# Two products of the second pair of f tiles moved into the first walk over D, with three f tiles of the first weights loaded at once

## The chip, the cores and the metric

One core of one Trainium2 chip. The time is device microseconds of one execution; runs are quoted by their median, and none was judged to be in a slow state (granted TensorE clock 0.999 or 1.0 in all but three runs, one each of e1, e3 and e6 below, at 0.996 to 0.997). Ratios are the mean time of one kernel's runs over the mean of the other's of the same rounds, so not quite the ratio of the medians. The span in a profile is some 1.8 us shorter than the time.

The readings come from one profiled execution of each kernel. The moment at which a load lands differs from one execution to the next, with equal loads too. The start of what is called "the train" below, which hangs on one such load, lies between 13.14 and 13.92 us in the six traces with the loads of before (mean 13.45). A difference of up to 0.8 us between two traces can therefore be chance.

## The reference

```python
# x [1, 2048, 1024], w_gate and w_up [1024, 3584], w_down [3584, 1024], all bf16
def reference(x, w_gate, w_up, w_down):
    return (gelu_tanh(x @ w_gate) * (x @ w_up)) @ w_down
```

## The kernel before

The 2048 tokens are done in two halves of 1024, each as two blocks of 512. The 3584 columns of the weights (f) are 28 tiles of 128, the 1024 of D are 8 blocks of 128. The first pair of f tiles is done by plain matmuls ("units": 64 matmuls for two f tiles, two token blocks, gate and up). Every later pair is a 2x2 block product done by Strassen's scheme in its Winograd form: 7 products of half size, M1 to M7, in place of 8. It needs sums of blocks of x ("t1" to "t4", made by VectorE with one cast on ScalarE) and of weights ("s1" to "s4", mostly by GpSimd). M1 and M2 use unsummed blocks: they are 16 bf16 matmuls on the first token block and the first f tile of the pair.

`pe`, `dve`, `act`, `sp` and `pool` fix the order of instructions on each engine. `banks` are the pieces of PSUM that TensorE writes its products to. Index `j` is 0 for gate and 1 for up. Cuts are marked with "...".

```python
FA = 2 * P                                    # two f tiles of the first weights at once
load_x0(0, sp, 0, 2); load_x0(0, act, 2, TSB) # x, D blocks 0-1, transposed on TensorE
load_w(first, 0, 0, 2, sp, 0, FA)             # gate, D blocks 0-1
load_x0(1, act)                               # x, D blocks 2-3
load_w(first, 1, 0, 2, sp, 0, FA)
load_w(first, 0, 2, 5, act, 0, FA)
load_w(first, 1, 2, 5, sp, 0, FA)
...                                           # 7 warming matmuls
load_xT(xT, 0, 0, KH, KH + 1)                 # x, D block 4, transposed by DMA, on SP
load_xT(xT, 0, 0, KH + 1, KH + 2)             # block 5
for j in range(2):
    load_w(first, j, 5, KD, act, 0, FA)       # D blocks 5-7, behind the first transpose
load_xT(xT, 0, 0, KH + 2, KD)                 # blocks 6-7
for k0, k1 in ((0, 2), (2, KH), (KH, KD)):    # x of the second 512 tokens
    load_xT(xT, 0, 1, k0, k1)
for j in range(2):
    load_w(first, j, 0, KD, sp, FA, FG)       # the other two f tiles

def first_pair_units(hT):
    held = (VB, RB)
    transpose_x0(0); ...
    part(held, 0, 0, KPQ, js=(0,))            # first 512 tokens, D blocks 0-1, gate
    transpose_x0(1)
    part(held, 0, 0, KPQ, js=(1,))
    part(held, 0, KPQ, KD)                    # the other D blocks
    t_sum("t1", 0, KH // 2); t_sum("t1", KH // 2, KH)
    for u in range(2):
        unit_out(hT, held[u], u, 0)           # gelu on ScalarE, multiply on VectorE
    held = (QB, PB)                           # fresh banks
    part(held, 1, 0, KH)                      # second 512 tokens
    t_sum("t2"); t_sum("b22"); t_sum("t3", 0, KH // 2)
    part(held, 1, KH, KD, (0,))
    unit_out(hT, held[0], 0, 1)
    t_sum("t3", KH // 2, KH)
    part(held, 1, KH, KD, (1,))
    unit_out(hT, held[1], 1, 1)
    for j in range(2):
        s_sum(0, 1, j, "s3", True, False)     # on VectorE
    for name in ("s1", "s2", "s4"):
        for j in range(2):
            s_sum(0, 1, j, name)              # on GpSimd

# pair_quads, second pair: M1, copies, M2, then M5 M5 M6 M6 M7 M7 M3 M3 M4 M4.
# t4 is made in halves: one ahead of M6's adds, one behind them.
def add_m5(dst, src):                         # VectorE; M4 needs it to be done
    dve(nc.vector.tensor_tensor(out=banks[dst][:], in0=banks[src][:],
                                in1=m5[j][:], op=ALU.add))
```

## Time and profile before

| | |
|---|---|
| time, median | 540.11 us (539.84 to 540.45, 3 runs); 539.65 with three more |
| span of the profiled execution | 538.0 us |
| TensorE busy | 532.4 us, 99% |
| second pair starts | 19.6 us |
| second pair's last product, M4, starts | 30.57 us |
| third pair starts | 32.52 us |
| each pair from the fourth on | 12.56 us (the third 10.83) |

Most of the kernel is a stream of matmuls without a gap, so anything lost or won in the first 33 us moves the end by as much. The prediction below shows the lines of this stage. GpSimd's timeline (start, length, engine, line, operation, out<-in, count, idle time before it):

```profile
18.39 4.03 POOL L385 TENSOR_TENSOR s_mem<-w_mem 128x512 fp32r<-128x512 bf16 x2 [17.08 <-DMA w_mem<-in_w_gate_dram]
22.38 3.19 POOL L385 TENSOR_TENSOR s_mem<-s_mem,w_mem 128x512 fp32r<-128x512 f32 x2
25.52 3.30 POOL L385 TENSOR_TENSOR s_mem<-w_mem,s_mem 128x512 fp32r<-128x512 bf16 x2
```

Two halves of t sums on VectorE in the same trace:

```profile
18.09 1.22 DVE L259 TENSOR_TENSOR t_mem<-xT 128x1024 fp32r<-128x1024 bf16 x1
25.06 1.59 DVE L259 TENSOR_TENSOR t_mem<-xT,t_mem 128x1024 fp32r<-128x1024 bf16 x1
```

### The profile page before, as it was taken

How to read it: one execution, taken by the hardware profiler on the slowest of the kernel's cores; microseconds unless marked ns; L12 is line 12 of the kernel's file. 1: busy time of each engine (PE TensorE's matmuls, PEld its weight loads, DVE VectorE, ACT ScalarE, POOL GpSimd, SP SyncE). 2: the span in 40 equal slices, each digit the busy share in tenths (PEclk: the TensorE clock that was granted, in tenths of full speed). 3: DMA queues.
4: the chain of work that ended last, by engine and by line, in shares of the span. 5: the costliest groups of instructions: out<-in, count | busy, mean ns of one | idle time of the engine just before them, and what ended most of it. 6: DMA issues, size and time to landing. Idle time of an engine off the chain costs nothing.

```text
span 538.0 us, 7084 instructions
## 1 busy us (share of the span) xinstructions
PE 532.4 (99%) x2352; PEld 377.9 (70%) x2388; DVE 364.2 (68%) x476; ACT 263.5 (49%) x447; POOL 244.4 (45%) x212
## 2 busy tenths in 40 slices
PE   9999999999999999999999999999999999999997
PEld 4577776666776686777776677777777766866866
DVE  1988777788775997989574334444444469969861
ACT  2555555555555329117465555555555552462280
POOL 0699877777776000000056776666777730000000
PEclk9999999999999999999999999999999999999999
DMA  9946876785815977789950405041322448677846
GB/s 205 323 128 195 207 252 185 238 262 197 291 61 200 361 239 246 237 279 308 324 171 1 156 1 158 15 142 57 100 78 80 155 133 284 220 246 252 293 141 212
DMA packets 92547, 102.70 MB, mean 191 GB/s; under 512 B 18656, under 2 KB 67424, under 8 KB 92512
## 3 DMA queue, kind: packets, MB, share of 16 engines
q1 hardware_dynamic: 69568, 80.23, 46.0%
q10 hardware_dynamic: 22944, 22.02, 13.4%
q8 instruction: 19, 0.31, 0.2%
q14 instruction: 16, 0.13, 0.1%
HBM read 85.98 MB, written 12.58 MB: 183 GB/s over the span
## 4 chain that ended last, share of the span: by engine, by line
PE 99%; issue 0%; ACT 0%; ACTq 0%
PE bank L413 63%; PE bank L703 33%; PE bank L264 3%; PE bank L202 1%; PE bank L308 0%; ACT bank L468 0%; ACT o_sb L759 0%; ACTq L468 0%
## 5 line engine op out<-in xcount | busy, mean ns | idle before, releaser
L413 PE MATMUL bank<-t_mem,s_mem 128*128 128x512 f32 x1056 | 249.6, 394 | 0.0
L413 PEld LDWEIGHTS bank<-t_mem,s_mem 128*128 128x128 f32 x1056 | 198.1, 188 | 44.1 <-DVE bank L436 0.4
L385 POOL TENSOR_TENSOR s_mem<-w_mem 128x512 fp32r<-128x512 bf16 x102 | 120.3, 1201 | 190.7 <-DVE t_mem L259 102.8
L703 PE MATMUL bank<-t_mem,s_mem 128*128 128x512 f32 (+1 forms) x548 | 127.2, 391 | 0.0
L288 DVE TENSOR_TENSOR hT<-w_mem,bank 128x512 bf16<-128x512 f32 x104 | 71.3, 687 | 79.9 <-PE bank L413 45.7
L703 PEld LDWEIGHTS bank<-t_mem,s_mem 128*128 128x128 f32 x548 | 102.4, 188 | 22.1 <-issue 0.2
L436 DVE TENSOR_TENSOR bank<-bank,m 128x512 f32<-128x512 f32 x108 | 69.9, 694 | 45.2 <-ACT m L458 43.7
L413 PE MATMUL bank<-xT,w_mem 128*128 128x512 bf16 x405 | 96.5, 380 | 1.4
L283 ACT ACTIVATE w_mem<-bank 128x512 f32<-128x512 f32 x104 | 61.8, 596 | 52.9 <-DVE bank L436 35.8
L413 PEld LDWEIGHTS <-w_mem 128*128 128x128 bf16 x432 | 40.2, 98 | 51.6 <-issue 6.8
L385 POOL TENSOR_TENSOR s_mem<-w_mem,s_mem 128x512 fp32r<-128x512 bf16 x52 | 65.8, 1285 | 0.0
L605 DVE TENSOR_TENSOR t_mem<-w_mem 128x1024 fp32r<-128x1024 bf16 x56 | 65.6, 1219 | 0.0
L385 POOL TENSOR_TENSOR s_mem<-s_mem,w_mem 128x512 fp32r<-128x512 f32 x52 | 60.9, 1192 | 0.0
L464 ACT COPY bank<-bank 128x512 f32<-128x512 f32 x54 | 30.8, 570 | 38.9 <-PE bank L413 38.9
L398 ACT CAST s_mem<-w_mem 128x512 fp32r<-128x512 bf16 x54 | 33.1, 615 | 30.6 <-PE bank L413 29.1
L675 DVE TENSOR_TENSOR s_mem<-hT 128x512 fp32r<-128x512 bf16 x52 | 34.2, 686 | 10.2 <-PE bank L703 9.4
L458 ACT COPY m<-bank 128x512 f32<-128x512 f32 x54 | 31.8, 589 | 17.5 <-PE bank L413 17.5
L703 PEld LDWEIGHTS <-hT 128*128 128x128 bf16 x224 | 21.3, 98 | 26.6 <-issue 2.1
L468 ACT COPY bank<-bank 128x512 f32<-128x512 f32 x54 | 30.7, 570 | 12.7 <-PE bank L413 12.7
L630 DVE TENSOR_TENSOR o_sb<-wd_sb,o_sb 128x512 fp32r<-128x512 bf16 x28 | 31.5, 1126 | 0.5
L768 ACT CAST o_sb<-bank 128x512 bf16<-128x512 f32 x27 | 14.8, 585 | 33.9 <-PE bank L703 33.9
L602 ACT CAST t_mem<-w_mem 128x1024 fp32r<-128x1024 bf16 x28 | 26.9, 1048 | 0.0
(45 smaller groups left out, 238.6 us busy)
## 6 DMA issues: line engine op xcount, KB each, us to landing
t_mem<-t_dram SPq DMA_DIRECT2D x56, 512.0 KB, 5.2
w_mem<-in_w_gate_dram ACTq DMA_DIRECT2D x10, 1024.0 KB, 5.5
w_mem<-in_w_up_dram ACTq DMA_DIRECT2D x10, 1024.0 KB, 5.5
wd_sb<-in_w_down_dram SPq DMA_DIRECT2D x28, 256.0 KB, 4.5
t_dram<-o_sb SPq DMA_DIRECT2D x28, 256.0 KB, 2.4
wd_sb<-in_w_down_dram SPq DMA_DIRECT2D x12, 512.0 KB, 7.7
w_mem<-in_w_down_dram SPq DMA_DIRECT2D x4, 1024.0 KB, 6.6
w_mem<-in_w_down_dram SPq DMA_DIRECT2D x8, 512.0 KB, 8.3
```

The lines of the kernel that those rows point to most:

```text
L283: act(nc.scalar.activation(out=g_sb, in_=ps[:], func=ACT.Gelu_apprx_tanh))
L288: nc.vector.tensor_tensor(out=hT[:, fc, tb * TB : (tb + 1) * TB], in0=g_sb, in1=ps[:], op=ALU.mult,)
L385: pool(nc.gpsimd.tensor_tensor(out=t, in0=in0, in1=in1, op=op))
L398: act(nc.scalar.copy(out=t, in_=a(1, 1)))
L413: nc.tensor.matmul(banks[bank][:], lhsT=lhs[:, c, :], rhs=rhs[:, c, :], start=start and c == 0, stop=c == KH - 1, skip_group_check=True,)
L436: nc.vector.tensor_tensor(out=banks[dst][:], in0=banks[src][:], in1=m5[j][:], op=ALU.add)
L458: act(nc.scalar.copy(out=m5[j][:], in_=banks[V_[j]][:]))
L464: act(nc.scalar.copy(out=banks[RB[j]][:], in_=banks[QB[j]][:]))
L605: dve(nc.vector.tensor_tensor(out=t, in0=in0, in1=in1, op=ALU.subtract))
L630: dve(nc.vector.tensor_tensor(out=t, in0=in0, in1=in1, op=ALU.subtract))
L675: dve(nc.vector.tensor_tensor(out=t, in0=in0, in1=in1, op=op))
L703: nc.tensor.matmul(banks[bank][:, c0:c1], lhsT=lhs(i, u), rhs=rhs(i)[:, c0:c1], start=start and i == 0, stop=stop and i == NS - 1, skip_gr ...
```

## The change

Its intent: while the first blocks of x arrive, each landed block should feed more matmuls. M1 and M2 of the second pair use the same x blocks as the units of the first 512 tokens, so they are done in the same walk over D. For this the third f tile has to come with the first two. The fourth comes with them for D blocks 5 to 7, and late for the others.

```diff
-    FA = 2 * P
+    FA = 3 * P
+    KA = 5
...
-        load_w(first, j, 5, KD, act, 0, FA)
+        load_w(first, j, KA, KD, act)                # all four f tiles, D blocks 5-7
...
-        load_w(first, j, 0, KD, sp, FA, FG)
+        load_w(first, j, 0, KA, sp, FA, FG)          # fourth f tile, D blocks 0-4
...                                                   # copies of x's transposes all on VectorE
-        held = (VB, RB)
+        held = (PB, RB)
+        def m12(j, k0, k1):                          # M1 into QB, M2 into VB
+            for kd in range(k0, k1):
+                pe(nc.tensor.matmul(banks[(QB, VB)[kd // KH][j]][:], ...))
...
-        part(held, 0, 0, KPQ, js=(1,))
-        part(held, 0, KPQ, KD)
...                                                   # M1 of D blocks 0-1
+        for j in range(2):
+            part(held, 0, KPQ, KH, js=(j,))
+            m12(j, KPQ, KH)
+            act(nc.scalar.copy(out=banks[VB[j]][:], in_=banks[QB[j]][:]))
+        for kd in range(KH, KD - 2):
+            part(held, 0, kd, kd + 1)
+            for j in range(2):
+                m12(j, kd, kd + 1)
...
         for u in range(2):
             unit_out(hT, held[u], u, 0)
-        held = (QB, PB)
-        part(held, 1, 0, KH)
+        for j in range(2):
+            m12(j, KD - 2, KD)
+        unit_out(hT, VB, 2, 0)                       # the multiply of M2, now ahead of t2
+        for j in range(2):
+            part(held, 1, 0, KH, js=(j,))            # the same banks again
         t_sum("t2")
...                                                   # pair_quads: M1 and M2 left out for this pair
```

More of the change, by code (lines that the diff above doesn't have):

```diff
@@ L303, in transpose_x0 @@
             parts = [(0, 0, 2), (0, 2, 4), (1, 0, 4)]
-        for n, (kd, ts0, ts1) in enumerate(parts):
-            tp = banks[(PB + QB)[(2 * q + n) % 4]][:].bitcast(BF16)
+        else:
+            parts.reverse()
+        for bank, (kd, ts0, ts1) in zip((PB[1], RB[1], QB[1])[q:], parts):
+            tp = banks[bank][:].bitcast(BF16)
             for ts in range(ts0, ts1):
@@ L314, in transpose_x0 @@
             cols = slice(ts0 * P, ts1 * P)
-            if q == 0 or n == 0:
-                dve(nc.vector.tensor_copy(out=xT[0][:, kd, cols], in_=tp[:, cols]))
-            else:
-                act(nc.scalar.copy(out=xT[0][:, kd, cols], in_=tp[:, cols]))
+            dve(nc.vector.tensor_copy(out=xT[0][:, kd, cols], in_=tp[:, cols]))
     def part(held, tb, k0, k1, us=(0, 1), js=(0, 1)):
@@ L326, in first_pair_units @@
     def first_pair_units(hT):
-        held = (VB, RB)
+        held = (PB, RB)
+        def m12(j, k0, k1):
+            for kd in range(k0, k1):
+                pe(
+                    nc.tensor.matmul(
+                        banks[(QB, VB)[kd // KH][j]][:],
+                        lhsT=block((0, "p", 1), j, 0, kd // KH)[:, kd % KH, :],
+                        rhs=xT[0][:, kd, :],
+                        start=kd == 0,
+                        stop=kd in (KH - 1, KD - 1),
+                        skip_group_check=True,
+                    )
+                )
         transpose_x0(0)
-        warm(RB[1], TB // 2)
+        warm(PB[0], TB // 2)
         part(held, 0, 0, KPQ, js=(0,))
+        m12(0, 0, KPQ)
         transpose_x0(1)
-        part(held, 0, 0, KPQ, js=(1,))
-        part(held, 0, KPQ, KD)
+        for u in range(2):
+            part(held, 0, 0, KPQ, (u,), (1,))
+        m12(1, 0, KPQ)
+        for j in range(2):
[7 more added lines that the diff above has]
+        for j in range(2):
+            part(held, 0, KD - 2, KD, js=(j,))
         t_sum("t1", 0, KH // 2)
@@ L338, in first_pair_units @@
             unit_out(hT, held[u], u, 0)
-        held = (QB, PB)
-        part(held, 1, 0, KH)
+        for j in range(2):
+            m12(j, KD - 2, KD)
+        unit_out(hT, VB, 2, 0)
+        for j in range(2):
+            part(held, 1, 0, KH, js=(j,))
         t_sum("t2")
@@ L464, in do_m6 @@
             act(nc.scalar.copy(out=banks[RB[j]][:], in_=banks[QB[j]][:]))
-        for j in range(2):
-            mm(P_[j], j, block(key, j, 0, 0), b11, True)
-            act(nc.scalar.copy(out=banks[QB[j]][:], in_=banks[P_[j]][:]))
         behind = len(pending) > 0
         eager = not behind and "m2" in then
+        if not eager:
+            for j in range(2):
+                mm(P_[j], j, block(key, j, 0, 0), b11, True)
+                act(nc.scalar.copy(out=banks[QB[j]][:], in_=banks[P_[j]][:]))
         if behind:
@@ L482, in pair_quads @@
         elif eager:
-            m2()
             done("m2")
```

## The prediction

> **What bounds the kernel now.** I read the page first (busy time and groups), then the chain of work at the start, then the table of stretches, then the timelines of VectorE and of the weight loads in the first 33 us, the only stage that the change touches.
>
> ```profile
> PE 532.4 (99%) x2352; PEld 377.9 (70%) x2388; DVE 364.2 (68%) x476; ACT 263.5 (49%) x447; POOL 244.4 (45%) x212
> ...
> L413 PE MATMUL bank<-t_mem,s_mem 128*128 128x512 f32 x1056 | 249.6, 394 | 0.0
> ```
>
> TensorE is busy 99% of 538.0 us, so time goes down only if matmuls are removed or a wait of TensorE is. In the raw trace a bf16 matmul of 512 columns starts every 216 ns (the 38 below: 8.36 us / 38 = 0.220, one record missing), and an f32 one every 227 ns. Once the pairs run behind each other, one takes 12.56 us, every time: 40 x 0.2267 + 16 x 0.2159 = 12.52. Nothing is to be had there.
>
> ```profile
> 6.55 4.43 PE bank L264 x20
> 10.98 0.02 issue
> 11.00 0.38 PE bank L264
> 11.38 0.05 issue
> 11.43 8.36 PE bank L264 x38
> ```
>
> In this chain of the start TensorE hardly waits either. Start to start, the matmul at 7.35 is 0.11 us late (weights landed 7.31), the one at 11.00 is 0.19 us late (the transpose of x for D blocks 6 and 7 landed 10.96). So the start waits 0.3 us in all, though it lives from hand to mouth: each load lands within half a microsecond of its use.
>
> ```profile
> 2.00:6.00 4.00, 4.00 (x20) 1.87 (x19) 0.96 (x3) 0.24 (x1) 0.00 (x0) 1.00 1.01 272
> 6.00:11.00 5.00, 4.98 (x29) 2.26 (x28) 0.42 (x1) 1.63 (x2) 0.00 (x0) 1.00 1.28 245
> 11.00:16.00 5.00, 4.94 (x23) 2.28 (x24) 3.68 (x5) 1.43 (x3) 0.00 (x0) 1.00 0.91 201
> 16.00:20.00 4.00, 4.00 (x20) 1.83 (x19) 4.00 (x4) 2.82 (x6) 1.61 (x1) 1.00 1.14 322
> 20.00:26.00 6.00, 5.95 (x28) 3.86 (x27) 6.00 (x6) 4.16 (x8) 6.00 (x5) 1.00 1.09 359
> ```
>
> The table of stretches (columns: length, then busy PE, PEld, DVE, ACT, POOL, clock, DMA share, GB/s) shows two other limits: the DMA engines are full from 2 to 11 us (share over 1), and VectorE is busy all of 16 to 26 us.
>
> ```profile
> 13.54 1.23 DVE L259 TENSOR_TENSOR t_mem<-xT,xT 128x1024 fp32r<-128x1024 bf16 x1 [0.19 <-DMA xT<-in_x_dram]
> ...
> 27.57 0.70 DVE L436 TENSOR_TENSOR bank<-bank,m 128x512 f32<-128x512 f32 x1 [0.22 <-ACT bank L464]
> 28.18 1.73 DVE L259 TENSOR_TENSOR t_mem<-xT,t_mem 128x1024 fp32r<-128x1024 bf16 x1
> 29.83 1.28 DVE L436 TENSOR_TENSOR bank<-bank,m 128x512 f32<-128x512 f32 x2
> ```
>
> ```profile
> 26.67 0.76 PEld L413 LDWEIGHTS bank<-t_mem,s_mem 128*128 128x128 f32 x4 [0.17 <-ACT bank L464]
> 27.59 2.59 PEld L413 LDWEIGHTS bank<-t_mem,s_mem 128*128 128x128 f32 x12 [0.15 <-ACT bank L464]
> 30.57 1.69 PEld L413 LDWEIGHTS bank<-t_mem,s_mem 128*128 128x128 f32 x8 [0.40 <-DVE bank L436]
> ```
>
> This is what I rest on. VectorE starts the second half of the sum t1 at 13.54, when x of the second 512 tokens has landed (13.42), and then works without a pause, but for 0.22 us, to the add that ends at 30.52. M4 of the second pair starts at 30.57, on that add. The two waits for ACT before are about 0.13 us each beyond the usual pace, the one for VectorE 0.36 us.
>
> **What the Trainium skill says.** "TensorE: Matmul & The Clock Gate", Back-to-back issue gap, gives N/2.4 + 2.5 ns, 216 ns for 512 columns; the trace has 216. "DMA: Bandwidth & Descriptors", Issuing engines are not separate DMA queues, says that DMAs from SP and ACT share the same 16 engines and interleave; the trace agrees, the total staying at 272 and 245 GB/s while both queues move data. The same page, Latency and other measured facts, gives 261 GB/s for a DMA transpose that cannot concatenate; in the trace they reach about 290 at best. "SBUF — State Buffer", Who interferes with whom, says that a VectorE instruction with two SBUF inputs contends with a GpSimd one that reads SBUF; the halves of t sums take 1.23 us before GpSimd starts (18.39) and 1.58 to 1.73 beside it.
>
> **The change, part by part.**
> (1) *Arithmetic.* M1 and M2 of the second pair are 16 matmuls, moved ahead, not removed. The order of instructions of both programs shows the same number of rows on TensorE. Work saved: none. The 32 matmuls of the first 512 tokens become 48 done in one walk over D, so each landed block of x feeds 6 matmuls in place of 4.
> (2) *Weights.* The first loads carry 3 f tiles in place of 2, and blocks 5 to 7 of D all 4. Extra before the transposes of the second 512 tokens: 2 x 65.5 KB (blocks 0, 1), 2 x 98.3 KB (2 to 4), 2 x 196.6 KB (5 to 7) = 721 KB. The late loads shrink by the same. At 322 to 359 GB/s, which plain weight loads reach in the last two stretches, that is 2.0 to 2.2 us of full DMA time.
> (3) *Does TensorE starve?* Needs after the change: first matmul 4.85 as before; blocks 2, 3 at 4.85 + 0.21 (cold) + 12 x 0.216 + 0.45 (transposes) = 8.1; block 4 at 10.7; block 5 at 12.0, its up weights 12.4; block 6 at 13.3. Arrivals, each moved by the extra bytes that I count in front of it: gate weights 2 to 4 at 7.3 + 0.8 = 8.1; up weights 5 to 7 at 10.1 + 2.0 = 12.1; x blocks 6, 7 at 10.96 + 1.9 = 12.9. So the need moves out about as far as the supply: no large wait, with 0.3 to 0.4 us to spare, and the old 0.3 us gone. That alone would save up to 0.3 us.
> (4) *VectorE.* The x of the second half comes behind all of it. On SP's own queue 229 KB are added ahead of it (0.7 us at 330 GB/s), on both 721 KB (2.2 us). I take 1.5 us: t1's second half starts at 15.0, not 13.54. VectorE's sequence from there to the add that M4 waits for has the same instructions (one multiply has moved forward, which changes no sum): 30.52 - 13.54 - 0.22 = 16.76 us of work. 15.0 + 16.8 = 31.8. The t4 half would end after GpSimd's burst and can win back up to 0.5 us: 31.3 to 31.8, against 30.52. TensorE arrives there at about 30.0, and waits. Cost: 0.8 to 1.3 us, which covers the early savings rather than adding to them.
> (5) *Banks.* The second 512 tokens now write the same banks (0, 1, 6, 7) as the first; before they had fresh ones. Four matmuls of M2 (0.86 us) and 8 more lie between, and gelu and multiply take 0.60 and 0.68 us each. The multiplies stand behind t1's second half: 15.0 + 1.23 + 2 x 0.65 = 17.5; bank 1 is needed at about 17.6. That holds narrowly.
> (6) *GpSimd.* It waits for the fourth tile, which lands about when it did (18.3, 20.0): later in the queue, but 164 KB in place of 524. No change. ACT swaps two bank copies for two others and loses one copy of x. No change.
> Sum: -0.3 at the start, which the later wait absorbs, and about +1.0 from VectorE: 540.1 + 1.0 = 541.1 if all of this holds.
>
> **The rivals.** *A, the plain gain:* the extra bytes hide, x of the second half lands as before, and the 0.3 us at the start and part of the 0.36 us before M4 vanish: 539.5. For it: the late weights get smaller, so GpSimd may start sooner and be out of VectorE's way; between 11 and 16 us DMA is not full (0.91). Against: it is full until 11. *B, TensorE starves:* the ACT queue, which gets 490 KB of the extra, falls behind, and the up weights of blocks 5 to 7 or the gate weights of 2 to 4 come 0.5 us or more after 12.4 and 8.1: 541 to 541.5, visible as a wait between 8 and 13.5 us. For it: 0.3 us to spare is less than my error. *C, mine:* VectorE's train starts late and M4, perhaps M3 too, waits. *D, C and the banks:* the full 2.2 us of delay, and the multiplies hold bank 1 too: 542.
>
> **Range and chances.** A at 0.3, B at 0.2, C at 0.4 (541.1), D at 0.1. Weighed: 0.3 x 539.5 + 0.2 x 541.2 + 0.4 x 541.1 + 0.1 x 542 = 540.7, and I round up to 540.8, as C is what I can show. None moves the time by 1%, and 2% is 10.8 us, the time of 48 matmuls, which are neither added nor removed. Runs of before spread by 0.6 us. Predicted 540.8, range 539.4 to 542.1; faster by over 2% 0.01, within 0.98, slower 0.01.
>
> **What would show it.** Right: the same count of matmuls; x of the second half landing 1 to 2 us later; t1's second half starting near 15.0; the add before M4 of the second pair ending past 31.2 with TensorE waiting over 1 us on it or on the adds before M3; pairs of 12.56 us from then on. Wrong: M4 of that pair starting before 30.5 (A), or a wait of over 0.5 us between 8 and 13.5 us (B). If any pair after the second runs at another pace, I have misread the whole.

## The result, and the profile after

The changed kernel takes 542.71 us (542.42 to 544.09, 6 runs), the kernel before 539.65 us (539.11 to 540.45, 6 runs): ratio 1.006, 95% interval 1.0046 to 1.0074. That is about 3 us slower, 0.6%. It lies within 2%, as I said, but outside my range, which ended at 542.1.

The profiled execution was the slowest of the six (544.09 us). Its span is 4.3 us longer than that of before. 3.4 us of it are there when the third pair starts; 0.8 us more are one late load near 493 us that the other traces do not show. The pairs from the fourth on again take 12.56 us each.

The stretches (columns as in the prediction: length, busy PE, PEld, DVE, ACT, POOL, clock, DMA share, GB/s):

```profile
6.00:11.00 5.00, 5.00 (x29) 2.50 (x28) 0.76 (x2) 1.01 (x2) 0.00 (x0) 1.00 1.22 242
11.00:16.00 5.00, 5.00 (x24) 2.15 (x23) 1.18 (x1) 1.65 (x3) 0.00 (x0) 1.00 1.08 215
26.00:33.00 7.00, 5.51 (x22) 3.83 (x23) 7.00 (x7) 1.66 (x3) 6.01 (x4) 1.00 0.32 116
```

TensorE does not starve up to 16 us. DMA is now full to 16 us (share 1.08, where it was 0.91), and in that stretch VectorE works 1.18 us in place of 3.68. From 26 to 33 us VectorE is busy all the time while TensorE is idle for 1.5 us of 7.

VectorE's timeline (L260 is the line of the t sums, L259 before; L465 the adds, L436 before):

```profile
16.31 1.22 DVE L260 TENSOR_TENSOR t_mem<-xT,xT 128x1024 fp32r<-128x1024 bf16 x1 [0.26 <-DMA xT<-in_x_dram]
17.45 1.88 DVE L289 TENSOR_TENSOR hT<-w_mem,bank 128x512 bf16<-128x512 f32 x3
19.24 2.28 DVE L260 TENSOR_TENSOR t_mem<-xT,t_mem 128x2048 fp32r<-128x2048 bf16 x1
21.45 2.18 DVE L260 TENSOR_TENSOR t_mem<-xT 128x1024 fp32r<-128x1024 bf16 x1
...
28.80 2.19 DVE L260 TENSOR_TENSOR t_mem<-xT,t_mem 128x1024 fp32r<-128x1024 bf16 x1
30.91 1.28 DVE L465 TENSOR_TENSOR bank<-bank,m 128x512 f32<-128x512 f32 x2
32.11 1.21 DVE L260 TENSOR_TENSOR t_mem<-xT,t_mem 128x1024 fp32r<-128x1024 bf16 x1
33.24 1.28 DVE L465 TENSOR_TENSOR bank<-bank,m 128x512 f32<-128x512 f32 x2
```

I call "the train" what VectorE does from the start of t1's second half to the end of the first add of the last row above, which frees the bank that M4 writes. Before it ran from 13.54 to 30.52 us, 16.98 us long. Now it runs from 16.31 to 33.93, 17.62 us, with no pause in it. The start moved by 2.77 us and the length by 0.64: together the 3.41 us by which the third pair starts later (35.93 against 32.52). Two halves of sums that took 1.22 and 1.59 us take 2.18 and 2.19 (the first half of t3, the first of t4). A third, t4's second half, took 1.73 and takes 1.21; the 0.64 us is what is left of all these and of shorter pauses.

The weight loads on TensorE show its waits in the second pair:

```profile
24.70 0.76 PEld L442 LDWEIGHTS bank<-t_mem,s_mem 128*128 128x128 f32 x4 [0.30 <-POOL s_mem L414]
26.80 0.76 PEld L442 LDWEIGHTS bank<-t_mem,s_mem 128*128 128x128 f32 x4 [1.33 <-POOL s_mem L414]
28.37 1.69 PEld L442 LDWEIGHTS bank<-t_mem,s_mem 128*128 128x128 f32 x8 [0.81 <-POOL s_mem L414]
...
33.98 1.69 PEld L442 LDWEIGHTS bank<-t_mem,s_mem 128*128 128x128 f32 x8 [0.58 <-DVE bank L465]
```

M4 starts at 33.98, on VectorE's add, as before. But TensorE also waits three times for GpSimd's sums (L414, L385 before), which it did not do before. GpSimd's timeline:

```profile
19.36 5.29 POOL L414 TENSOR_TENSOR s_mem<-w_mem 128x512 fp32r<-128x512 bf16 x2 [18.06 <-DMA w_mem<-in_w_gate_dram]
24.61 3.71 POOL L414 TENSOR_TENSOR s_mem<-s_mem,w_mem 128x512 fp32r<-128x512 f32 x2
28.29 3.73 POOL L414 TENSOR_TENSOR s_mem<-w_mem,s_mem 128x512 fp32r<-128x512 bf16 x2
```

The six sums start 1.0 us later, and take 12.7 us in place of 10.4. The first of the six alone, and the second:

```profile
19.36 3.18 POOL L414 TENSOR_TENSOR s_mem<-w_mem 128x512 fp32r<-128x512 bf16 x1 [18.06 <-DMA w_mem<-in_w_gate_dram]
22.50 2.15 POOL L414 TENSOR_TENSOR s_mem<-w_mem 128x512 fp32r<-128x512 bf16 x1
```

Read beside VectorE's lines, the two engines take turns. t2 ends at 21.53; GpSimd's first sum, begun before, ends 1.02 us after that, at 22.55; the first half of t3, begun at 21.45, ends 1.08 us after that, at 23.63; GpSimd's second sum ends 1.02 us after that, at 24.65. It goes on so to the end of GpSimd's work at 32.01: six turns of GpSimd of 1.01 to 1.03 us and five of VectorE's sums (three of 1.08, two of 0.55 us) add up to the whole 10.49 us. VectorE's multiplies and adds, which read one operand from PSUM, take no turn: 0.67 to 0.69 us beside GpSimd and 0.68 alone.

So the trace leaves several candidates: the late x (L), the order and the banks (O), the port to SBUF at which VectorE and GpSimd take these turns (P), and GpSimd's sums being late for TensorE (G).

### The profile page after: what moved, and what is told of

Same layout as the page of the kernel before. It is cut to its first block, busy times and chain, and to the rows that moved or that the text cites.

```text
span 542.3 us, 7127 instructions
## 1 busy us (share of the span) xinstructions
PE 536.4 (99%) x2388; PEld 377.9 (70%) x2388; DVE 365.0 (67%) x477; ACT 262.8 (48%) x446; POOL 246.5 (45%) x212
## 4 chain that ended last, share of the span: by engine, by line
PE 95%; DVE 2%; DMA 1%; issue 1%; ACT 0%; DVEq 0%
PE bank L442 61%; PE bank L732 31%; PE bank L265 1%; DMA t_mem<-t_dram 1%; DVE t_mem L260 1%; PE bank L333 1%; PE bank L203 1%; DVE hT L289 0%; DVE s_mem L412 0%; DVE bank L465 0%; PE bank L311 0%; ACT o_sb L788 0%; DVEq L289 0%; DVEq L260 0%
## 5 line engine op out<-in xcount | busy, mean ns | idle before, releaser
L414 POOL TENSOR_TENSOR s_mem<-w_mem 128x512 fp32r<-128x512 bf16 x102 | 121.6, 1213 | 192.1 <-DVE t_mem L260 103.0
L465 DVE TENSOR_TENSOR bank<-bank,m 128x512 f32<-128x512 f32 x108 | 69.8, 694 | 44.9 <-ACT m L487 43.7
L442 PE MATMUL bank<-xT,w_mem 128*128 128x512 bf16 x416 | 94.3, 380 | 0.0
L442 PEld LDWEIGHTS <-w_mem 128*128 128x128 bf16 x416 | 38.6, 98 | 49.7 <-issue 6.8
L414 POOL TENSOR_TENSOR s_mem<-w_mem,s_mem 128x512 fp32r<-128x512 bf16 x52 | 66.3, 1301 | 0.0
L414 POOL TENSOR_TENSOR s_mem<-s_mem,w_mem 128x512 fp32r<-128x512 f32 x52 | 61.2, 1198 | 0.0
L493 ACT COPY bank<-bank 128x512 f32<-128x512 f32 x54 | 30.8, 570 | 40.7 <-PE bank L442 40.7
L500 ACT COPY bank<-bank 128x512 f32<-128x512 f32 x52 | 29.6, 570 | 11.7 <-PE bank L442 11.7
```

Of the source, the lines that this page charges most:

```text
L414: pool(nc.gpsimd.tensor_tensor(out=t, in0=in0, in1=in1, op=op))
L442: nc.tensor.matmul(banks[bank][:], lhsT=lhs[:, c, :], rhs=rhs[:, c, :], start=start and c == 0, stop=c == KH - 1, skip_group_check=True,)
L493: act(nc.scalar.copy(out=banks[RB[j]][:], in_=banks[QB[j]][:]))
```

## The experiments

All times of one batch stand beside the kernel before on the same chip. Fourteen kernels ran. "Train" is read from each trace as above. Six runs compute a wrong result on purpose, marked in the table; the other eight are correct.

| run | early bytes added | train starts | train length | third pair starts | time, us | ratio (95% interval) |
|---|---|---|---|---|---|---|
| before | 0 | 13.54 | 16.98 | 32.52 | 539.65 | |
| changed | 721 KB | 16.31 | 17.62 | 35.93 | 542.71 | 1.0060 (1.0046 to 1.0074) |
| e1_loads_only | 721 KB | 15.69 | 17.03 | 34.72 | 542.33 | 1.0049 (1.0024 to 1.0074) |
| d_half_dose | 393 KB | 14.66 | 17.02 | 33.68 | 541.07 | 1.0028 (1.0013 to 1.0043) |
| e2_order_only (wrong) | 0 | 13.47 | 19.28 | 34.76 | 542.31 | 1.0039 (1.0023 to 1.0055) |
| p_before (wrong) | 0 | 13.21 | 16.98 | 32.47 | 539.58 | 0.9997 (0.9980 to 1.0014) |
| p_after (wrong) | 721 KB | 16.37 | 14.39 | 33.09 | 540.15 | 1.0011 (0.9996 to 1.0025) |
| p_order (wrong) | 0 | 13.43 | 16.95 | 32.70 | 539.21 | 0.9994 (0.9979 to 1.0009) |
| q_after (wrong) | 721 KB | 16.20 | 17.62 | 35.82 | 543.57 | 1.0070 (1.0055 to 1.0085) |
| q_order (wrong) | 0 | 13.14 | 19.29 | 34.43 | 542.30 | 1.0049 (1.0032 to 1.0066) |
| e3_weights_first | 721 KB | 15.45 | 17.62 | 35.08 | 542.88 | 1.0062 (1.0032 to 1.0092) |
| e4_mult_late | 721 KB | 15.56 | 17.29 | 34.85 | 542.61 | 1.0051 (1.0034 to 1.0068) |
| e5_fourth_late | 524 KB | 14.78 | 17.60 | 34.39 | 541.69 | 1.0039 (1.0022 to 1.0056) |
| e6_fourth_ahead | 1049 KB | 18.75 | 16.17 | 36.95 | 543.75 | 1.0077 (1.0062 to 1.0092) |
| b3_weights_first | 0 | 14.26 | 17.02 | 33.28 | 540.12 | 1.0010 (0.9995 to 1.0025) |
| b4_mult_late | 0 | 13.92 | 16.96 | 32.88 | 539.65 | 1.0001 (0.9986 to 1.0016) |

### The loads alone

```diff
 # kernel before
-    FA = 2 * P
+    FA = 3 * P
+    KA = 5
-        load_w(first, j, 5, KD, act, 0, FA)
+        load_w(first, j, KA, KD, act)
-        load_w(first, j, 0, KD, sp, FA, FG)
+        load_w(first, j, 0, KA, sp, FA, FG)
```

> The order of the kernel before with the loads of the changed one. If the larger early loads are the cause (theory L: x of the second 512 tokens lands late, VectorE's train starts late, M4 of the second pair waits), nearly the whole loss is here: 542 to 543 us, t1's second half starting near 16. If the order of the matmuls and the re-used banks are the cause (theory O): 539.5 to 540.

Measured: 542.33 us. The third pair starts 2.20 us later. The train starts 2.15 us later (15.69), and its length is the old one (17.03). That the length is the same is the sum of changes that cancel: t3's first half is stretched here too, while the pause of 0.22 us is gone and t4's second half is short (1.21 us).

```profile
20.23 2.18 DVE L260 TENSOR_TENSOR t_mem<-xT 128x1024 fp32r<-128x1024 bf16 x1
28.18 1.60 DVE L260 TENSOR_TENSOR t_mem<-xT,t_mem 128x1024 fp32r<-128x1024 bf16 x1
```

TensorE had even waited 1.9 us for x of D block 5, which landed at 12.32, and that wait cost nothing on top: the train had not reached M4 by then. L holds for the loads, with GpSimd's sums in place.

### Half of the extra bytes

```diff
 # kernel before
-        load_w(first, j, 5, KD, act, 0, FA)
+        load_w(first, j, 5, KD, act)
-        load_w(first, j, 0, KD, sp, FA, FG)
+        load_w(first, j, 0, 5, sp, FA, FG)
```

> The kernel before with all four f tiles of blocks 5 to 7 loaded early: 393 KB more ahead of x of the second 512 tokens, against 721 in the run with all loads of the change. If bytes set the landing: t1's second half at 14.6 to 15.0 (13.5 before, 15.7 with all), and 540.7 to 541.3. If bytes are not it, but the slow service of ACT's large packets beside transposes: as late as with all, 15.5, as the large packets on ACT are all here, and 542.

Measured: 541.07 us, the train starting at 14.66. In the order of before, three doses (0, 393, 721 KB) give starts at 13.54, 14.66 and 15.69, lengths of 16.98, 17.02 and 17.03, and third pairs at 32.52, 33.68 and 34.72. In these traces each microsecond of delay of x delays the third pair by about one. The bytes on both queues count in full: 393 KB / 1.12 us = 351 GB/s, 721 KB / 2.15 us = 335 GB/s, the rate of plain weight loads in the table of stretches (322 to 359). From the means of all traces with these loads, the delay of 721 KB is 16.03 - 13.45 = 2.6 us (280 GB/s), so the rate is known only roughly. The large packets on ACT are all in this dose, and about half the bytes gave about half the delay, so they need no explanation of their own.

### The order alone

```diff
 # changed kernel; the loads of before, and
-    lhsT=block((0, "p", 1), j, 0, kd // KH)[:, kd % KH, :],
+    lhsT=block((0, "p", 0), j, 0, kd // KH)[:, kd % KH, :],
```

> The order of the changed kernel with the loads of before; M1 and M2 of the second pair take the weights of another f tile that is there early, so the result is wrong on purpose. Theory L: 539.2 to 540.0, t1's second half near 13.5. Theory O: 542 or more.

Measured: 542.31 us, against L. x landed as before and the train starts at 13.47, but it is 19.28 us long. VectorE's timeline:

```profile
15.12 1.91 DVE L288 TENSOR_TENSOR hT<-w_mem,bank 128x512 bf16<-128x512 f32 x3 [0.43 <-PE bank L264]
16.95 2.29 DVE L259 TENSOR_TENSOR t_mem<-xT,t_mem 128x2048 fp32r<-128x2048 bf16 x1
19.15 2.18 DVE L259 TENSOR_TENSOR t_mem<-xT 128x1024 fp32r<-128x1024 bf16 x1
21.74 0.69 DVE L288 TENSOR_TENSOR hT<-w_mem,bank 128x512 bf16<-128x512 f32 x1 [0.41 <-ACT w_mem L283]
22.34 2.19 DVE L259 TENSOR_TENSOR t_mem<-xT 128x1024 fp32r<-128x1024 bf16 x1
```

The multiplies of the first 512 tokens stand ahead of t2, and with 12 more matmuls ahead of them on TensorE they wait for it (0.43 us). A third multiply has joined them. So t2 starts at 16.95, not 15.88. GpSimd starts its sums at 17.89 here. Before, the first half of t3 began at 18.09, ahead of GpSimd, and took 1.22 us. Here it begins at 19.15, behind GpSimd's start, and takes 2.18. By the start of the third pair the order costs 2.2 us by itself, and the loads 2.2 us by themselves; together 3.4 us, not 4.4. The two costs overlap: the stretch of t3's first half is in both runs and counts once, and a late x hides the wait for TensorE (in the changed kernel the multiplies wait for nothing).

With x late, what the order adds is one item. Between e1 (17.03 us) and the changed kernel (17.62) every entry of the train agrees to 0.05 us but two: the multiply of M2, 0.6 us, stands ahead of t2 and no longer between s3 and t4's first half, and that half takes 2.19 us, not 1.60. Where the multiply stood it ran in a turn of GpSimd's and cost nothing; ahead of t2, where GpSimd has not begun, it costs its own length.

That VectorE's sums are longer because GpSimd is in the way was so far read off one trace's times. The next runs test it.

### GpSimd's six sums taken away

```diff
+    for name in ("s1", "s2", "s4"):
+        for j in range(2):
+            pool(nc.gpsimd.memset(s_fixed(j, name).bitcast(F32), 0.01))   # at the start
...
-                s_sum(0, 1, j, name)
+                ssum[(0, 1, j, name)] = s_fixed(j, name).rearrange("p (a b) -> p a b", b=P)
```

The tiles that M5, M6 and M3 of the second pair read are constants set in the first microseconds, so GpSimd does nothing from then until the third pair's sums, and the result is wrong. This was done to the kernel before, the changed one, and the one with the order alone.

> The kernel before, with GpSimd's six sums for the second pair (s1, s2, s4) taken away: those tiles are set to a constant at the start, so the result is wrong on purpose. Theory P: from 18 to 32 us VectorE's train of sums is stretched by GpSimd, which holds up each VectorE instruction with two SBUF inputs, and that stretched train sets M4 of the second pair. Then the train here ends 1.5 to 2.5 us sooner, and the time falls only by the 0.36 us that M4 waits: 539.0 to 540.0. Theory L (the landing of x alone matters): the same as before.

> The changed kernel with the same six sums taken away (wrong on purpose). Theory P: t1's second half still starts near 16, but the train then takes about 14 us in place of 17.6, M4 starts at 30 to 31, and the time is 539.5 to 540.5, nearly all of the loss gone. Theory L: at most 0.7 us of the loss goes, 542 or more.

> The run with the changed order and the loads of before, with the same six sums taken away (wrong on purpose). Theory P: the order alone costs 2.2 us because the multiplications of the first 512 tokens wait for TensorE, push t2 and t3 into GpSimd's sums and so stretch the train; without those sums 539.0 to 540.0. If the order costs in another way (banks, TensorE's own order): still 541.5 or more.

Measured: 539.58, 540.15 and 539.21 us. The changed kernel loses 0.11% in place of 0.60%, and the order alone 0 in place of 0.39%. VectorE's timeline in p_after:

```profile
21.51 1.22 DVE L260 TENSOR_TENSOR t_mem<-xT 128x1024 fp32r<-128x1024 bf16 x1
...
26.30 1.22 DVE L260 TENSOR_TENSOR t_mem<-xT,t_mem 128x1024 fp32r<-128x1024 bf16 x1
...
30.07 1.29 DVE L475 TENSOR_TENSOR bank<-bank,m 128x512 f32<-128x512 f32 x2
```

x is as late as ever (the train starts at 16.37), but the train is 14.39 us long, not 17.62, because the sums take 1.22 us again. In p_before the train should have ended at least 1.5 us sooner, and it ended only 0.3 us sooner (30.19), all of it from an earlier start. Pauses filled its length: VectorE waits 1.06 us for TensorE and 1.47 us for ScalarE, which are then the slower ones. So in the kernel before GpSimd's sums had already used up VectorE's slack, and any delay of the train showed.

These runs took away two things at once: GpSimd's use of the port, and TensorE's waits for its sums. They also give VectorE some 3 us of slack, in which a late start or another wait can hide; so they show that the loss needs GpSimd's sums, and not that the sums are all of it. No run has the late x in the old order without the sums.

### The port kept busy, the waits taken away

```diff
 # p_after, p_order
+                idle_sum(j, name)     # the same six sums on GpSimd, into tiles nobody reads
                 ssum[(0, 1, j, name)] = s_fixed(j, name).rearrange(...)
```

> The changed kernel with GpSimd doing the same six sums at the same time, but into tiles that nobody reads; TensorE reads constants set at the start, as in the runs without the sums (wrong on purpose). So the shared port is as busy as ever, and no wait of TensorE for GpSimd is left. Theory P (the port stretches VectorE's train, and the train sets M4): train 17 to 17.6 us, 542.2 to 543. Theory G (TensorE's waits for GpSimd's late sums set the time): as without the sums, 540.2.

> The same for the changed order with the loads of before (wrong on purpose). Theory P: train 18.5 to 19.3 us, 541.3 to 542.5. Theory G: 539.2.

Measured: 543.57 and 542.30 us, the full loss again. In q_after:

```profile
28.69 2.19 DVE L260 TENSOR_TENSOR t_mem<-xT,t_mem 128x1024 fp32r<-128x1024 bf16 x1
31.60 1.69 PEld L470 LDWEIGHTS bank<-t_mem,s_mem 128*128 128x128 f32 x8 [1.96 <-issue]
33.87 1.69 PEld L470 LDWEIGHTS bank<-t_mem,s_mem 128*128 128x128 f32 x8 [0.58 <-DVE bank L493]
```

TensorE no longer waits for GpSimd at all, and reaches M3 sooner, to wait there 1.9 us in q_after (the view names no releaser; M3 starts 0.12 us after an add on VectorE ends, as in the changed kernel and in e2). The trains have the old lengths to 0.01 us (17.62 and 19.29). G is refuted. P is shown: GpSimd's work beside VectorE's sums, and not the arrival of what it makes, is what the loss needs. The constants that TensorE reads are the same as in the p runs, so they are not what took the loss away there. That it is GpSimd's reading of SBUF that collides, and not its writing, no run separates.

### Attempts to shorten the train or to speed up the loads

```diff
 # e3: changed kernel; b3: the same in the kernel before
+    for j in range(2):
+        load_w(first, j, KA, KD, sp)
     load_xT(xT, 0, 0, KH, KH + 1)
...
-        load_w(first, j, KA, KD, act)
```

> The changed kernel with the weights of blocks 5 to 7 issued from SP ahead of the transposes of x, not from ACT beside them. If the part of the delay that I did not foresee (2.8 us measured against 2.2 us of bytes) comes from transposes and weights being served side by side (theory M), x of the second half lands 1 to 2 us sooner and the time is 540.5 to 541.7. If bytes alone count: 542.5 or more, as the bytes ahead of that x are the same.

> The kernel before with the weights of blocks 5 to 7 issued from SP ahead of the transposes. x of blocks 6 and 7 lands 0.3 to 1 us sooner, as it did in the changed kernel, x of the second half at most 0.5 us sooner: 539.2 to 539.8, the 0.19 us wait for x gone if block 4 does not come late (after 9.1).

Measured: 542.88 us in the changed kernel. x of D blocks 6 and 7 came 1.3 us sooner (12.12), but x of the second half only 0.85 us sooner than in the profile of the changed kernel and 0.2 us sooner than in e1, whose loads are those of the changed kernel. The larger of the two is about what traces with equal loads differ by, and the time did not improve. So the gain of 1 to 2 us from no longer serving transposes and weights side by side did not show. In the kernel before the same move gave 540.12 us, no gain, with x of the second half 0.7 us later (14.14), where I had expected it at most 0.5 us sooner.

```diff
 # e4: changed kernel; b4: the same in the kernel before
-        unit_out(hT, VB, 2, 0)
+        g_m2 = gelu(banks[VB[0]])
+        late.append(lambda: mult(hT, g_m2, banks[VB[1]], 2, 0))   # run behind M7's adds
```

> The changed kernel with the multiplication of the second pair's M2 output moved from ahead of t2 to behind the adds of M7, out of VectorE's train. If the train sets the start of M4 (theory L): about 0.6 us faster, 542.1. If the sums on GpSimd set it (theory G), or the banks: no change, 542.7.

> The kernel before with the multiplication of the second pair's M2 output moved out of VectorE's train, behind the adds of M7. If the count of VectorE instructions in the train sets M4: its 0.36 us of waiting goes and the time is 539.2. If the port shared with GpSimd sets it: the multiplication, which reads PSUM, is no port work, the wait stays within 0.2 us, and the time is as before.

Measured: 542.61 and 539.65 us. Taking a multiply of 0.68 us out shortens the train by 0.33 us in the changed kernel and by 0.02 us in the one before. In the changed kernel 0.2 us of it became a wait, because t2's x had not landed. In the kernel before, t4's first half began 0.6 us sooner, counted from the start of the train, and met more of GpSimd's sum: 2.19 us in place of 1.59. The multiply reads one operand from PSUM and had run beside GpSimd at no cost. The time moves less than a run's noise; it is the trace that decides. I had expected 0.6 us from it in the changed kernel.

```diff
 # e5: changed kernel, the fourth f tile late for all D blocks
-    KA = 5
+    KA = KD
-        load_w(first, j, KA, KD, act)
+        load_w(first, j, 5, KD, act, 0, FA)
 # e6: changed kernel, the late weights ahead of x of the second 512 tokens
-    for k0, k1 in ((0, 2), (2, KH), (KH, KD)):
-        load_xT(xT, 0, 1, k0, k1)
     for j in range(2):
         load_w(first, j, 0, KA, sp, FA, FG)
+    for k0, k1 in ((0, 2), (2, KH), (KH, KD)):
+        load_xT(xT, 0, 1, k0, k1)
```

> The changed kernel with the fourth f tile late for all blocks of D: 197 KB fewer ahead of x of the second 512 tokens, the same bytes more behind it. Theory L (landing of x): t1's second half 0.5 to 0.7 us sooner, near 15.5, and the time 542.0. Theory P (landing and shared port together): GpSimd's sums also start later, near 20, which takes back part: 542 to 543.

> The changed kernel with the late weights (the fourth f tile) loaded ahead of x of the second 512 tokens. Theory L: that x lands about 1 us later still, 543.5 to 544. Theory P: GpSimd starts some 3 us sooner, so more of its sums are done before the train meets them: 542 to 543, no worse than the changed kernel.

Measured: e5 takes 541.69 us. 197 KB fewer ahead of x, and the train starts at 14.78, as long as before the edit (17.60). GpSimd did not start later (18.49, where I had expected 20), so what I expected to be taken back was not. e6 takes 543.75 us, as L said and against what I wrote for P. GpSimd starts at 15.48 and the train is shorter (16.17), but it starts at 18.75. Also, TensorE waits 2.6 us at 18.7 us for the multiply that frees bank 1. So an earlier start of GpSimd does not pay for a later x.

No version beat the kernel before beyond the noise. The changed kernel's best variant (e5) still loses 0.4%.

## Why the prediction was wrong

By its own steps:

- **What bounds the kernel**, and that the only stage to look at is the first 33 us: right. The pairs from the fourth on kept 12.56 us. One reading was too general: not every load landed within half a microsecond of its use (x of D block 4 landed at 8.06 and was used about 9.1). It did no harm. The bound inside that stage was named as well: VectorE's train from the landing of x to M4. Every run shows M4 starting within 0.1 us of the end of the train, except the three without GpSimd's sums, in which TensorE is the slower one.
- **(1) and (3), matmuls and starving**: right that TensorE does not starve. In the profile after, TensorE up to 16 us waits once, 0.15 us, for x of D block 5 (landed 12.74). The up weights of blocks 5 to 7 landed at 12.66, where I had 12.1, and x of blocks 6 and 7 at 13.38, not 12.9. They were in time because TensorE itself was late: four of its first matmuls started 427 ns apart, where before only one did, which is 0.6 us. A wait of this size (1.9 us in e1) did not reach M4 in any case. Rival B is out.
- **(4), the delay of x, failed in size.** I had 0.7 us from the bytes on SP's own queue and 2.2 us from the bytes on both, and took 1.5 in between. Measured: 2.77 us in the profiled execution, 2.15 in e1 with the same loads, 2.6 in the mean of the five traces with them. The two-queue figure was the right term. The page that I quoted says that the queues share the 16 engines, and I had seen the engines full up to 11 us, so nothing spoke for the middle. d_half_dose shows that the ACT queue's bytes count in full.
- **(4), the length of the train, failed outright.** I took 16.76 us of work as a constant ("one multiply has moved forward, which changes no sum") and let up to 0.5 us of it be won back. It was 17.62. The 0.5 us was won (t4's second half, 1.21 in place of 1.73 us), but t3's first half lost 0.96 us and t4's first half 0.60. The durations in it depend on whether GpSimd is at the port at that moment, which I had quoted from the SBUF page myself without using it. x came 2.8 us later and GpSimd began only 1.0 us later, which put the first half of t3 behind GpSimd's start (e1 has this too). And the moved multiply did change a sum: t4's first half now waits out the turn of GpSimd in which the multiply used to run. The order alone costs 2.2 us (e2). Without GpSimd's sums that cost is not there (p_order: 0), with them it is all back (q_order). Not all of it is longer sums: e2's trace also has two waits of VectorE, 0.43 us for TensorE and 0.41 for ScalarE, which the slack of p_order can hide.
- The end of the train was therefore 33.93 and not 31.3 to 31.8. Of the 2.1 to 2.6 us missing, 1.3 are the start (16.31 against 15.0) and 0.8 to 1.4 the length (17.62 against 16.76, or 16.3 with the win-back).
- **(5), banks**: held, as I had it, narrowly; only in e6, with x later still, did bank 1 make TensorE wait.
- **(6), GpSimd, "no change"**: wrong. It started 1.0 us later and its six sums took 12.7 us in place of 10.4, for the same reason seen from the other side.
- **Rivals**: C was the right mechanism as far as the late train goes, at a size beyond D's; the sums stretched by GpSimd were in no rival. A was given 0.3 for the hope that bytes hide; they did not. The range ended at 542.1 because the delay and the stretch were never added.

## What to carry to other kernels

When a change loads more ahead of something, charge all bytes in front of it on every queue (here at 280 to 351 GB/s), and ask which engine starts late, not whether TensorE starves. Do not carry durations of VectorE's sums over from a trace when GpSimd works beside them: look up when GpSimd starts and ends, and which instructions will newly fall into that stretch. While both have such sums queued, the sum of their turns is the length to plan with (10.49 us here, from 21.53 to 32.01 us). Work that takes no turn, here a multiply that reads PSUM, is free inside that stretch and costs its length ahead of it; taking it out of the train won 0.33 and 0.02 us (e4, b4).

## What the Trainium skill lacked or had wrong

- "SBUF — State Buffer", Who interferes with whom: the rule held, and it gives no durations for sums like these. A VectorE sum of 128x1024 bf16 took 1.22 us alone and up to 2.20 us beside GpSimd (q_order), a GpSimd sum of 128x512 1.16 us alone and up to 3.21 us (e6). The page says that the second to issue blocks until the first is done; in a train this makes the engines take turns (here of 1.08 and 1.02 us), and the six sums on GpSimd lengthened VectorE's train by 3.2 us (17.62 against 14.39), nearly half of GpSimd's own 7.0 us (an estimate: 6 x 1.16).
- "DMA: Bandwidth & Descriptors", Latency and other measured facts: 261 GB/s for a DMA transpose that cannot concatenate. Between 14.0 and 14.75 us, when only packets of transposes moved in the kernel before, the trace has 290 GB/s; over 12 to 13.4 us, at a DMA share of 0.80, only 174. No page gives a size for how long SP is held by issuing transposes: the six issues took 10.44 us before and 13.03 after, with 721 KB more in front of the later ones. Why is not shown.
- "TensorE: Matmul & The Clock Gate", Back-to-back issue gap: 216 ns for 512 columns holds for bf16 (216 in the trace). The section calls that the gap of an isolated matmul and gives about 131 ns for a stream; here the stream ran at 216. The f32 operands here run at 227 ns, which the page does not give.
